# Talking-heads attention followed by a parametric-ReLU feed-forward: half of each step's feed-forward share placed ahead of the score products, four rounded-half tiles for seven relay tiles, the first input split spread over three steps

## Chip, cores and metric

The kernel runs on 1 core of one Trainium2 chip. The metric is the device time of one launch in microseconds (us), the median of several runs.

## What is computed

Four batches, 12 heads, 448 tokens, head size 64; then a feed-forward over 1792 tokens with 768 model and 2048 hidden features. The inputs q, k and w_pre are drawn eight times larger than the other random tensors.

```
def _attn_ref(q, k, v, w_pre, w_post):
    scale = 1.0 / np.sqrt(q.shape[-1])
    scores = scale * np.matmul(q, k.transpose(0, 1, 3, 2))
    scores = np.einsum('bhij,hg->bgij', scores, w_pre)
    scores = scores - np.max(scores, axis=-1, keepdims=True)
    attn = np.exp(scores)
    attn = attn / (np.sum(attn, axis=-1, keepdims=True) + 1e-09)
    attn = np.einsum('bhij,hg->bgij', attn, w_post)
    return np.matmul(attn, v).astype(np.float32)

def _moe_ref(x, w_in, w_out, alpha):
    h = x @ w_in
    g = np.maximum(h, 0.0) + alpha * np.minimum(h, 0.0)
    return (g @ w_out).astype(np.float32)
```

The feed-forward's x is the attention's output with heads side by side. `w_in` and `w_out` come as 64-bit floats.

## The kernel before

There are two phases: attention, and the feed-forward. Attention goes in 90 steps. Queries are cut into 32 chunks of 60 rows (30 at a batch's end); a chunk has 6 (or 3) groups of 10 rows over 12 heads, and a step treats two groups. A step `n` (`step`, line 595) issues, in this order:

- `mix(n)` (L209): the pre-softmax head mixing, 8 matmuls on TensorE from two relay tiles `sr` into a pair of PSUM banks; then the row maximum `nm` on VectorE (L211).
- `relays` (L202): SyncE copies score rows from the chunk's tile `st` into a ring of 8 relay tiles `sr`, two DMAs a group. A tile is refilled when the mix that read it has ended.
- `flush`: SyncE stores finished output rows `xe` to the scratch `x2` in DRAM (L271).
- `norm(n-1)` on VectorE (L567 to L571); every sixth step or so `pv` (L254), the product with v; `post(n-2)` (L231), the post-softmax mixing, 56 matmuls, copied by ScalarE to `at` (L237).
- `exp(n)` on ScalarE (L218).
- one or two score products `qk` (L186) of a chunk some steps ahead, copied by ScalarE to `st` (L190), and the loads of q and k on ScalarE's queue.
- `moe_work`: a share of the feed-forward, in two halves, with `converts` behind each.

The share is set by `PACE`: 2000 modelled ns a step while the first batch's feed-forward runs, 5400 after it. `moe(t)` is a generator; each `next` issues 3 matmuls of the first layer (L409) or 12 of the second (L443) and returns a cost from 207 ns a matmul. The feed-forward of the first batch begins at step 29. What is left of it when the steps end runs alone.

The weights are float64 and are rounded to float32 on the chip in 64 units of 128x384 (`convert`, `round_f64`, lines 51 to 68), each in five instructions' worth of `next`: exponent mask on VectorE (L61); clamp and scale of the exponent on GpSimd (L62, L63) and mantissa mask on VectorE (L65); and three more on VectorE (L66 to L68). The result lies in a tile `ct`, of which there are 3, and GpSimd stores it to the scratch `wsc` (L297). That store is issued when the unit two later does its clamp, and behind the clamp:

```
            for j, op in enumerate(round_f64(nc, raw, e, t)):
                op()
                if j == 1 and shut:
                    shut.pop(0)()
                if j == 4:
                    shut.append(close)
                yield
```

A unit's tile is first written at L65, so VectorE stops there until the store of the unit three earlier has landed. The feed-forward loads `wr` back from `wsc` (L339); ScalarE rounds it (L352) and GpSimd subtracts (L353), which gives the two parts `ws` of a weight. `load_w` runs conversions ahead of their turn when its weight is not stored yet.

The feed-forward's input is read back from `x2` in six pieces `xr` of 128x448 (two buffers, SyncE, L459), each split by two VectorE instructions into `xs` (L472, L473). For the first batch all six are split at the end of step 27.

PSUM is four pairs of banks; a group takes the pair that was freed longest ago. Every engine works its own list in order, and SyncE's and ScalarE's DMA issues stand in those lists too.

Of the kernel before, what the change touches and what calls it, by code (L numbers as in the profile page):

```python
# [10 lines left out]
I32 = mybir.dt.int32  # L11
# [17 lines left out]
NCC = DM // 128  # L29
# [2 lines left out]
NS = 4  # L32
NJ = S // 64
SR0 = 4
RA = 4
QA = 3
NSR = 2 * RA
WARM = 12
LAG = 2
TB = [(b * S, S) for b in range(B)]  # L40
# [2 lines left out]
AW = 2 * CW  # L43
FG = 2
NG2 = NFC // FG
PACE = (2000.0, 5400.0, 5400.0)
CU = DM // 2
CONV_LEAD, CONV_T0 = 4, 4


def round_f64(nc, raw, e, t):

    w = raw.bitcast(I32).rearrange("p (n t) -> p n t", t=2)
    lo, hi = w[:, :, 0], w[:, :, 1]
    tf = t.bitcast(F32)
    v, g = nc.vector, nc.gpsimd

    yield lambda: v.tensor_scalar(out=e, in0=hi, scalar1=0x7FF00000, scalar2=None, op0=ALU.bitwise_and)  # L61
    g_clamp = lambda: g.tensor_scalar(out=e, in0=e, scalar1=float(1150 << 20), scalar2=float(916 << 20), op0=ALU.min, op1=ALU.max)  # L62
    g_scale = lambda: g.tensor_scalar(out=e, in0=e, scalar1=float(-(916 << 20)), scalar2=8.0, op0=ALU.add, op1=ALU.mult)  # L63
    yield lambda: (g_clamp(), g_scale(),
                   v.tensor_scalar(out=t, in0=hi, scalar1=0xFFFFF, scalar2=0x100000, op0=ALU.bitwise_and, op1=ALU.bitwise_or))  # L65
    yield lambda: v.scalar_tensor_tensor(out=tf, in0=lo.bitcast(U32), scalar=2.0 ** -32, in1=t, op0=ALU.mult, op1=ALU.add)  # L66
    yield lambda: v.scalar_tensor_tensor(out=e, in0=hi, scalar=-0x80000000, in1=e, op0=ALU.bitwise_and, op1=ALU.bitwise_or)
    yield lambda: v.tensor_tensor(tf, tf, e.bitcast(F32), ALU.mult)  # L68
# [3 lines left out]
def talking_heads_prelu(ctx: ExitStack, tc: tile.TileContext, q, k, v, w_pre, w_post, mask, w_in, w_out, alpha, out):  # L72
# [141 lines left out]
    def exp(n):  # L214
        e_t[n] = ep.tile([128, 2, S], F32, tag="e", name=f"e{n}")
        se_t[n] = sm.tile([128, 2], F32, tag="se", name=f"se{n}")
        for u in range(2):
            nc.scalar.activation(out=e_t[n][:, u], in_=m_t[n][:, u, :S], func=AF.Exp, bias=nm_t[n][:, u:u + 1], scale=1.0,  # L218
                                 accum_out=se_t[n][:, u:u + 1])
        free(m_t.pop(n))  # L220
# [59 lines left out]
    def convert():  # L280
        todo = [(f, x, c) for f in range(NFC) for x in range(2) for c in range(0, DM, CU)]
        raw_c, shut = {}, []

        def fetch_c(i):
            if i < len(todo):
                f, x, c = todo[i]
                raw_c[i] = cvp.tile([128, CU], I64, tag="cr", bufs=4, name=f"cr{f}_{x}_{c}")
                nc.gpsimd.dma_start(out=raw_c[i], in_=(w_in, w_out)[x][f, :, c:c + CU])

        def unit(i):  # L290
            f, x, c = todo[i]
            raw = raw_c.pop(i)
            e = cvp.tile([128, CU], I32, tag="ce", name=f"ce{f}_{x}_{c}")
            t = cvp.tile([128, CU], I32, tag="ct", bufs=3, name=f"ct{f}_{x}_{c}")
            def close():
                stored.add((f, x, c))
                nc.gpsimd.dma_start(out=wsc[f, :, x * DM + c:x * DM + c + CU], in_=t.bitcast(F32))  # L297
                fetch_c(i + 4)

            for j, op in enumerate(round_f64(nc, raw, e, t)):  # L300
                op()
                if j == 1 and shut:
                    shut.pop(0)()
                if j == 4:
                    shut.append(close)
                yield

        for i in range(2):
            fetch_c(i)
        yield  # L310
        n = len(todo)
        seq = []
        for i in range(n + 1):
            seq += [(i, 0), (i, 1), (i, 2)] if i < n else []
            seq += [(i - 1, 3), (i - 1, 4)] if i else []
        units = {}
        for i, j in seq:
            if j == 0:
                units[i] = unit(i)
            next(units[i], None)  # L320
            if i < 2 and j == 1:
                fetch_c(i + 2)
            yield
        for f in shut:
            f()


    wr_t, wi_t, wo_t, g_t, xs_t, xr_t = {}, {}, {}, {}, {}, {}
# [133 lines left out]
    def split_x(t):  # L462
        a, N = TB[t]
        while step_now[0] < ready[t] + 1:
            yield
        for c in range(2):
            if (t, c) not in xr_t:
                load_x(t, c)
        xs = xs_t[t] = xsp.tile([128, 2, NCC, N], F32R, tag="xs", name=f"xs{t}")
        for c in range(NCC):  # L470
            xr = xr_t.pop((t, c))
            nc.vector.tensor_copy(xs[:, 0, c, :], xr[:, :N])  # L472
            nc.vector.tensor_tensor(xs[:, 1, c, :], xr[:, :N], xs[:, 0, c, :], ALU.subtract)  # L473
            if c + 2 < NCC:
                load_x(t, c + 2)
            yield
# [20 lines left out]
    with tc.manual_schedule():  # L497
# [45 lines left out]
        def relays(upto, dmas):  # L543
            nonlocal relayed
            while relayed < min(upto, NG) and (groups[relayed][0], NP // 2 - 1) in done_qk:
                relay(relayed, dmas)
                relayed += 1

        relays(4, (nc.sync, nc.scalar))
        relays(2 * RA, (nc.sync,))  # L550
        next(conv)
        conv_done, conv_steps = 0, NFC * 2 * 5 * (DM // CU) + 1
        tasks = [None] * len(TB)
# [3 lines left out]
        def converts(n):  # L557
            nonlocal conv_done
            for _ in range(n):
                if conv_done < conv_steps:  # L560
                    next(conv, None)
                    conv_done += 1
# [12 lines left out]
        def moe_work(n, amount):  # L575
            nonlocal cur, budget
            budget += amount
            while budget > 0 and cur < len(TB):
                if tasks[cur] is None:
                    if n <= ready[cur] + 2:  # L580
                        budget = 0.0
                        return
                    for _ in (nxt_x[cur] if cur in nxt_x else split_x(cur)):
                        pass
                    if cur == 1:
                        converts(conv_steps)
                        cvs.close()
                        wops.append(ctx.enter_context(tc.tile_pool(name="wop2", bufs=2, reuse_waits="tile")))
                    tasks[cur] = moe(cur)
                try:  # L590
                    budget -= next(tasks[cur])
                except StopIteration:
                    cur += 1

        def step(n):
            step_now[0] = n
            due = pv_at.get(n)
            lead = n <= ready[0] + 2
            pace = 0.0 if lead else PACE[min(cur, 2)]
            if live(n):  # L600
                mix(n)
            if n >= 0:
                relays(2 * (n + RA + 1), (nc.sync,))
            flush()
            if live(n - 1):
                norm(n - 1)
            if due is not None:
                b = pvs[due][0]
                for hx in range(2):
                    pv(due, hx)  # L610
                    if due + 1 < len(pvs) and pvs[due + 1][0] != b:
                        load_v(b + 1, hx)
            if live(n - LAG):
                post(n - LAG)
            if live(n):
                exp(n)
            for ci, p in qk_at.get(n, []):
                b = chunks[ci][0]
                qk(ci, p)
                if ci + 1 < NC and chunks[ci + 1][0] != b:  # L620
                    load_k(b + 1, p)
                if p == 2 and ci + 3 < NC:
                    load_q(ci + 3)
            if n in (-1, 0):
                load_q(n + 3)
            if n in (2, 3):
                load_v(0, n - 2)
            if lead:
                converts(CONV_LEAD)
            else:  # L630
                moe_work(n, pace * 0.5)
                converts(CONV_T0 // 2 + n % 2)
                moe_work(n, pace * 0.5)
                converts(CONV_T0 - CONV_T0 // 2)
            for t in range(len(TB)):
                if n == ready[t] and t == 0:
                    load_x(t, 0)
                    load_x(t, 1)
                if n == ready[t] + 1 and t == 0:
                    for _ in split_x(0):  # L640
                        pass
                    nxt_x[0] = iter(())
            if n == ready[0] - 5:
                ahead(1)
                for u in range(2):
                    load_w(u, 1)
            if n == ready[0] - 2:
                for u in range(2):
                    split_w(u, 0)
                ahead(2)  # L650
# [43 lines left out]
```

## Time and profile before

| what | us |
|---|---|
| runs | 987.4 median of 3, 985.16 to 995.29 |
| profiled execution, its time | 984.49 |
| its span, first to last instruction | 982.7 |
| TensorE matmul busy | 856.1 (87%) |
| VectorE busy | 611.3 (62%) |
| GpSimd busy | 460.2 (47%) |
| ScalarE busy | 428.8 (44%) |

PE is TensorE, PEld its weight loads, DVE VectorE, ACT ScalarE, POOL GpSimd, SP SyncE; a q behind a name is its queue of DMA issues. A row of the timeline has start, length, engine, line, operation, tiles, count, and in brackets the idle time before it and what ended that. L12 is line 12 of the kernel. The attention steps reach from 22 to 634 us, and the feed-forward is mixed into them from 204 us on; from 634 us it runs alone.

### The profile page before, as it was taken

How to read it: one execution, taken by the hardware profiler on the slowest of the kernel's cores; microseconds unless marked ns; L12 is line 12 of the kernel's file. 1: busy time of each engine (PE TensorE's matmuls, PEld its weight loads, DVE VectorE, ACT ScalarE, POOL GpSimd, SP SyncE). 2: the span in 40 equal slices, each digit the busy share in tenths (PEclk: the TensorE clock that was granted, in tenths of full speed). 3: DMA queues.
4: the chain of work that ended last, by engine and by line, in shares of the span. 5: the costliest groups of instructions: out<-in, count | busy, mean ns of one | idle time of the engine just before them, and what ended most of it. 6: DMA issues, size and time to landing. Idle time of an engine off the chain costs nothing.

```text
span 982.7 us, 27239 instructions
## 1 busy us (share of the span) xinstructions
PE 856.1 (87%) x11532; PEld 670.0 (68%) x11532; DVE 611.3 (62%) x1079; ACT 428.8 (44%) x780; POOL 460.2 (47%) x532
## 2 busy tenths in 40 slices
PE   5688595488896889787989979999999999999997
PEld 2465364266574566555657758899988999889997
DVE  4468674488947686864846556546466465765464
ACT  2367483365564456453556645423323223133231
POOL 5224243137444455536330310666555766567661
PEclk8779897889999989899889989999999999999999
DMA  6677957767865865685574542443345443454322
GB/s 183 174 223 231 244 160 249 240 174 218 227 186 172 245 208 169 204 241 173 176 195 124 156 145 101 120 125 113 97 132 166 125 115 106 126 161 116 110 81 73
DMA packets 84234, 161.71 MB, mean 165 GB/s; under 512 B 27300, under 2 KB 68720, under 8 KB 84112
## 3 DMA queue, kind: packets, MB, share of 16 engines
q0 software_dynamic: 19968, 88.36, 31.9%
q1 hardware_dynamic: 48216, 55.59, 17.8%
q10 hardware_dynamic: 15928, 16.01, 6.4%
q8 instruction: 91, 1.49, 0.7%
q14 instruction: 31, 0.25, 0.1%
HBM read 97.62 MB, written 23.59 MB: 123 GB/s over the span
## 4 chain that ended last, share of the span: by engine, by line
PE 52%; DMA 16%; DVE 14%; issue 6%; POOL 6%; ACT 4%; ACTq 1%; SPq 1%; POOLq 0%; DVEq 0%
PE p L409 19%; PE p L443 17%; DMA sr<-st 7%; PE p L254 5%; PE p L231 5%; PE p L186 4%; POOL ws L353 4%; PE p L209 3%; DMA x<-xe 3%; DMA wsc<-ct 3%; DVE nm L211 2%; ACT e L218 2%; DVE acc L375 2%; DMA xr<-x 1%; DMA k<-in_k_dram 1%
## 5 line engine op out<-in xcount | busy, mean ns | idle before, releaser
L353 POOL TENSOR_TENSOR ws<-wr,ws 128x768 fp32r<-128x768 f32 x128 | 236.6, 1849 | 274.3 <-ACT ws L352 273.4
L443 PE MATMUL p<-g,ws 128*128 128x448 f32 x1152 | 250.2, 372 | 15.4 <-DVE t L361 6.9
L409 PE MATMUL p<-xs,ws 128*128 128x448 f32 x1152 | 250.8, 371 | 1.8 <-POOL ws L353 0.8
L443 PEld LDWEIGHTS p<-g,ws 128*128 128x128 f32 x1152 | 217.1, 190 | 47.1 <-DVE t L361 8.6
L409 PEld LDWEIGHTS p<-xs,ws 128*128 128x128 f32 x1152 | 214.0, 189 | 43.7 <-issue 18.5
L352 ACT CAST ws<-wr 128x768 fp32r<-128x768 f32 x128 | 104.1, 837 | 207.2 <-issue 117.0
L231 PEld LDWEIGHTS p<-r,e 64*64 64x64 f32 x5040 | 112.4, 148 | 79.4 <-ACT at L237 29.1
L231 PE MATMUL p<-r,e 64*64 64x60 f32 x5040 | 116.9, 236 | 36.3 <-ACT at L237 20.4
L218 ACT ACTIVATE e<-p,nm 128x448 f32<-128x448 f32 x180 | 112.9, 636 | 72.7 <-DVE nm L211 64.2
L237 ACT COPY at<-p 128x960 f32<-128x960 f32 x88 | 86.8, 986 | 118.9 <-PE p L231 67.7
L209 PE MATMUL p<-sr,wk 64*64 64x448 f32 (+1 forms) x720 | 103.6, 609 | 35.6 <-DMA sr<-st 11.0
L360 DVE TENSOR_SCALAR t<-p,alpha_sb 128x448 f32<-128x448 f32 x64 | 43.5, 679 | 143.2 <-PE p L409 143.2
L211 DVE TENSOR_REDUCE nm<-p 128x2 f32<-128x896 f32 x90 | 97.7, 1085 | 47.9 <-PE p L209 47.5
L186 PE MATMUL p<-k,q 64*64 64x448 f32 x768 | 110.3, 618 | 14.6 <-ACT at L237 6.1
L62 POOL TENSOR_SCALAR ce<-ce 128x384 int32<-128x384 int32 x64 | 34.8, 543 | 180.4 <-DVE ce L61 178.8
L375 DVE TENSOR_TENSOR acc<-p,acc 128x896 f32<-128x896 f32 x84 | 90.6, 1085 | 36.6 <-PE p L443 33.5
L254 PEld LDWEIGHTS p<-at,v 64*64 64x64 f32 x2688 | 79.2, 138 | 26.8 <-ACT e L218 20.1
L254 PE MATMUL p<-at,v 64*64 64x120 f32 (+1 forms) x2688 | 82.3, 269 | 16.3 <-ACT e L218 15.8
L339 POOL DMA_DIRECT2D wr<-wsc x128 | 71.9, 562 | 43.0 <-POOL ws L353 30.3
L190 ACT COPY st<-p 128x896 f32<-128x896 f32 x95 | 84.8, 915 | 13.0 <-PE p L186 6.9
L209 PEld LDWEIGHTS p<-sr,wk 64*64 64x64 f32 (+1 forms) x720 | 26.2, 142 | 74.8 <-ACT e L218 15.4
L367 DVE TENSOR_TENSOR g<-t,g 128x448 fp32r<-128x448 f32 x64 | 73.0, 1181 | 0.9 <-ACT g L366 0.9
(45 smaller groups left out, 591.4 us busy)
## 6 DMA issues: line engine op xcount, KB each, us to landing
wr<-wsc POOLq DMA_DIRECT2D x128, 384.0 KB, 3.4
sr<-st SPq DMA_DIRECT2D x356, 105.0 KB
cr<-in_w_in_dram POOLq DMA_DIRECT2D x32, 384.0 KB, 5.3
cr<-in_w_out_dram POOLq DMA_DIRECT2D x32, 384.0 KB, 5.1
wsc<-ct POOLq DMA_DIRECT2D x64, 192.0 KB, 3.9
xr<-x SPq DMA_DIRECT2D x24, 224.0 KB
out_dram<-acc SPq DMA_DIRECT2D x12, 448.0 KB
q<-in_q_dram ACTq DMA_DIRECT2D x53, 90.0 KB
```

The costliest lines, as they stand in the source:

```text
L186: nc.tensor.matmul(pt[64 * cc:64 * cc + 64, r, :S], q_t[ci][h, (3 * cc + p) * cn + (64 - cn) * cc:(3 * cc + p) * cn + (64 - cn) * cc + 64] ...
L209: nc.tensor.matmul(to[hf:hf + 64, u, :S], wk[r, :], g[r, :], start=True, stop=True)
L211: nc.vector.tensor_reduce(out=nm, in_=to[:, :, :S], axis=AX.X, op=ALU.max, negate=True)
L218: nc.scalar.activation(out=e_t[n][:, u], in_=m_t[n][:, u, :S], func=AF.Exp, bias=nm_t[n][:, u:u + 1], scale=1.0, accum_out=se_t[n][:, u:u ...
L231: nc.tensor.matmul(dst[:, :, HI * u:HI * u + HI], e[h, u, 64 * jb:64 * jb + 64], r[h, u].rearrange("p (h i) -> p h i", h=H), start=True, s ...
L237: nc.scalar.copy(at[:, :, col:col + 2 * GI].rearrange("p q (g i) -> p g q i", g=2), pt[:, :, :NS * GP].rearrange("p g (q i) -> p g q i", i ...
L254: nc.tensor.matmul(to[64 * t:64 * t + 64, r, cl * cn:(cl + 1) * cn], v_t[b, hx][pr, s, (2 * cl + t) * D:(2 * cl + t + 1) * D], a_t[pr, s, ...
L352: nc.scalar.copy(t[:, 0], w)
L353: nc.gpsimd.tensor_tensor(t[:, 1], w, t[:, 0], ALU.subtract)
L375: nc.vector.tensor_tensor(dst, pt[:, :, :N], dst, ALU.add)
L409: nc.tensor.matmul(pt[:, f % 2, :S], w[:, tw, c * 128:(c + 1) * 128], xs[:, tx, c, :], start=(j == 0), stop=(j == 3 * NCC - 1))
L443: nc.tensor.matmul(pt[:, d, :S], w[:, tw, (c + d) * 128:(c + d + 1) * 128], g[:, tg], start=(j == 0), stop=(j == 3 * FG - 1))
```

## The change

The relay ring has 7 tiles instead of 8, and step n asks for groups up to 2n+8 instead of 2n+9; `ct` has 4 tiles instead of 3; the store of a rounded unit stands ahead of the later unit's clamp, its next fetch behind it; PACE is 2100 for the first batch; the first feed-forward starts at step 30; half of a step's share stands between `post`/`exp` and `qk`, the other half behind `qk`; two of the conversions stand ahead of `qk`; the six pieces of the first input are split two each in steps 27, 28 and 29.

```diff
-RA = 4
-NSR = 2 * RA
+NSR = 7
-PACE = (2000.0, 5400.0, 5400.0)
+PACE = (2100.0, 5400.0, 5400.0)
...
-            t = cvp.tile([128, CU], I32, tag="ct", bufs=3, name=f"ct{f}_{x}_{c}")
+            t = cvp.tile([128, CU], I32, tag="ct", bufs=4, name=f"ct{f}_{x}_{c}")
             def close():
                 stored.add((f, x, c))
                 nc.gpsimd.dma_start(out=wsc[f, :, x * DM + c:x * DM + c + CU], in_=t.bitcast(F32))
+                yield
                 fetch_c(i + 4)
+                yield
 
             for j, op in enumerate(round_f64(nc, raw, e, t)):
+                if j == 1 and shut:
+                    next(shut[0])
                 op()
                 if j == 1 and shut:
-                    shut.pop(0)()
+                    next(shut.pop(0))
                 if j == 4:
-                    shut.append(close)
+                    shut.append(close())
...
-        relays(2 * RA, (nc.sync,))
+        relays(NSR, (nc.sync,))
...
-                    if n <= ready[cur] + 2:
+                    if n <= ready[cur] + 3:
...
-            lead = n <= ready[0] + 2
+            lead = n <= ready[0] + 3
...
-                relays(2 * (n + RA + 1), (nc.sync,))
+                relays(2 * (n + 1) + NSR, (nc.sync,))
...
             if live(n):
                 exp(n)
+            if not lead:
+                moe_work(n, pace * 0.5)
+            converts(CONV_LEAD // 2)
             for ci, p in qk_at.get(n, []):
...
-            if lead:
-                converts(CONV_LEAD)
-            else:
+            if not lead:
                 moe_work(n, pace * 0.5)
-                converts(CONV_T0 // 2 + n % 2)
-                moe_work(n, pace * 0.5)
-                converts(CONV_T0 - CONV_T0 // 2)
+            converts(CONV_LEAD // 2 + (0 if lead else n % 2))
...
-                if n == ready[t] + 1 and t == 0:
-                    for _ in split_x(0):
-                        pass
-                    nxt_x[0] = iter(())
+                if ready[t] < n <= ready[t] + 3 and t == 0:
+                    split0 = nxt_x.setdefault(0, split_x(0))
+                    for _ in range(NCC // 3):
+                        next(split0)
```

`ready[0]` is 26. Line numbers of the changed kernel differ by a few; in the pieces of its order below L208 is the mix, L230 post, L185 the score product, L412 the first layer, L210 the row maximum, L475 and L476 the split, L296 the store of a rounded unit, L61 and L62 its clamp and scale, and L287 the fetch.

On TensorE in step 31, before:

```order
L209 MATMUL p_130<-sr_123,wk 64x448 x2
L209 MATMUL p_130<-sr_124,wk 64x448 x2
L231 MATMUL p_132<-r_2696,e_2651 64x12x5 x28
L186 MATMUL p_131<-k_1_1410,q_126 64x448 x4
L409 MATMUL p_133<-xs_2426,ws_0_2120 128x448 x9
```

and in the same step now:

```order
L208 MATMUL p_131<-sr_123,wk 64x448 x2
L208 MATMUL p_131<-sr_117,wk 64x448 x2
L230 MATMUL p_132<-r_2674,e_2643 64x12x5 x28
L412 MATMUL p_129<-xs_2422,ws_0_2113 128x448 x6
L185 MATMUL p_130<-k_1_1413,q_125 64x448 x4
L412 MATMUL p_129<-xs_2422,ws_0_2116 128x448 x3
```

Six of the nine first-layer matmuls moved ahead of the score product (sr_117 to sr_124 are the relay tiles, now to sr_123, and p_129 to p_133 are PSUM pairs).

On GpSimd in the attention phase, one unit's pass, before:

```order
L62 TENSOR_SCALAR ce_1_0_1051<-ce_1_0_1051 128x384
L63 TENSOR_SCALAR ce_1_0_1051<-ce_1_0_1051 128x384
L297 DMA wsc<-ct_0_0_868 128x384
L288 DMA cr_0_0_1058<-in_w_in_dram 128x384
L62 TENSOR_SCALAR ce_1_384_1126<-ce_1_384_1126 128x384
```

and now:

```order
L296 DMA wsc<-ct_0_0_864 128x384
L61 TENSOR_SCALAR ce_1_0_1042<-ce_1_0_1042 128x384
L62 TENSOR_SCALAR ce_1_0_1042<-ce_1_0_1042 128x384
L287 DMA cr_0_0_1049<-in_w_in_dram 128x384
L296 DMA wsc<-ct_0_384_932 128x384
```

The store of the unit two earlier moved ahead of the clamp and scale; the fetch stayed behind them.

On VectorE from the end of step 27, before:

```order
L472 CAST xs_2426<-xr_0_2348 128x448
L473 TENSOR_TENSOR xs_2426<-xr_0_2348,xs_2426 128x448
L472 CAST xs_2426<-xr_1_2350 128x448
L473 TENSOR_TENSOR xs_2426<-xr_1_2350,xs_2426 128x448
L472 CAST xs_2426<-xr_2_2429 128x448
L473 TENSOR_TENSOR xs_2426<-xr_2_2429,xs_2426 128x448
L472 CAST xs_2426<-xr_3_2433 128x448
L473 TENSOR_TENSOR xs_2426<-xr_3_2433,xs_2426 128x448
L472 CAST xs_2426<-xr_4_2437 128x448
L473 TENSOR_TENSOR xs_2426<-xr_4_2437,xs_2426 128x448
L472 CAST xs_2426<-xr_5_2441 128x448
L473 TENSOR_TENSOR xs_2426<-xr_5_2441,xs_2426 128x448
```

and now, with the next row maximum in view:

```order
L475 CAST xs_2422<-xr_0_2346 128x448
L476 TENSOR_TENSOR xs_2422<-xr_0_2346,xs_2422 128x448
L475 CAST xs_2422<-xr_1_2348 128x448
L476 TENSOR_TENSOR xs_2422<-xr_1_2348,xs_2422 128x448
L210 TENSOR_REDUCE nm_2435<-p_131 128x2
L570 TENSOR_SCALAR s_2441<-se_2397 128x2
L571 RECIPROCAL s_2441<-s_2441 128x2
L574 TENSOR_TENSOR r_2444<-wq,s_2441 128x120
```

Two pieces stand ahead of step 28's row maximum instead of six.

## Rows read from the trace of the kernel before

**Rows 1.** Stretches: length, busy PE, PEld, DVE, ACT, POOL, PEclk, DMA share, GB/s
```profile
22.00:178.00 156.00, 114.70 (x2570) 73.63 (x2567) 97.09 (x223) 88.38 (x178) 52.11 (x89) 0.83 0.75 219
178.00:204.00 26.00, 12.52 (x361) 9.28 (x353) 15.36 (x37) 8.43 (x18) 5.78 (x11) 0.79 0.60 185
204.00:634.00 430.00, 375.75 (x6847) 270.43 (x6851) 289.06 (x565) 233.21 (x448) 176.96 (x232) 0.94 0.62 181
634.00:983.00 349.00, 340.35 (x1723) 310.12 (x1714) 201.22 (x230) 94.79 (x134) 211.73 (x174) 1.00 0.41 118
```

**Rows 2.** The chain that ended last, after 634 us: start, length, what
```profile
641.51 7.44 PE p L409 x36
```

**Rows 3.** Waits of VectorE from 204 to 634 us: total, times, longest
```profile
DVE ct L65 <- DMA wsc<-ct: 40.6, 13, 8.0
```

**Rows 4.** Timeline, VectorE at the first and last of four long waits
```profile
297.06 0.36 DVE L65 TENSOR_SCALAR ct<-cr 128x384 int32<-128x384 int32 x1 [8.03 <-DMA wsc<-ct]
...
465.31 0.36 DVE L65 TENSOR_SCALAR ct<-cr 128x384 int32<-128x384 int32 x1 [6.51 <-DMA wsc<-ct]
```

**Rows 5.** Timeline, TensorE ahead of and behind these waits
```profile
290.75 0.98 PE L209 MATMUL p<-sr,wk 64*64 64x448 f32 x8
291.55 1.04 PE L231 MATMUL p<-r,e 64*64 64x60 f32 x54
...
301.50 1.77 PE L209 MATMUL p<-sr,wk 64*64 64x448 f32 x8 [4.26 <-ACT e L218]
303.05 1.91 PE L231 MATMUL p<-r,e 64*64 64x60 f32 x56
...
310.30 1.09 PE L231 MATMUL p<-r,e 64*64 64x60 f32 x54 [2.83 <-DVE r L571]
...
344.80 1.86 PE L231 MATMUL p<-r,e 64*64 64x60 f32 x54 [5.10 <-ACT e L218]
...
397.34 1.77 PE L209 MATMUL p<-sr,wk 64*64 64x448 f32 x8 [3.76 <-ACT e L218]
...
468.23 2.24 PE L443 MATMUL p<-g,ws 128*128 128x448 f32 x5 [6.91 <-DVE t L361]
```

**Rows 6.** Timeline, GpSimd ahead of the first of them
```profile
289.42 0.51 POOL L62 TENSOR_SCALAR ce<-ce 128x384 int32<-128x384 int32 x1
290.01 0.52 POOL L63 TENSOR_SCALAR ce<-ce 128x384 int32<-128x384 int32 x1
290.58 0.59 POOL L297 DMA_DIRECT2D wsc<-ct  x1
```

**Rows 7.** Timeline, the split of the first input
```profile
184.96 0.63 DVE L473 TENSOR_TENSOR xs<-xr,xs 128x448 fp32r<-128x448 f32 x1
...
188.00 5.50 SPq L459 DMA_DIRECT2D xr<-x  x4
191.13 0.40 DVE L472 CAST xs<-xr 128x448 fp32r<-128x448 f32 x1 [5.55 <-DMA xr<-x]
...
199.55 3.41 PE L254 MATMUL p<-at,v 64*64 64x90 f32 x81 [12.03 <-ACT e L218]
...
207.65 1.09 DVE L211 TENSOR_REDUCE nm<-p 128x2 f32<-128x896 f32 x1 [1.13 <-PE p L209]
```

**Rows 8.** Timeline, VectorE beside a subtraction of GpSimd
```profile
230.50 2.03 POOL L353 TENSOR_TENSOR ws<-wr,ws 128x768 fp32r<-128x768 f32 x1 [4.01 <-ACT ws L352]
230.72 2.23 DVE L67 SCALAR_TENSOR_TENSOR ce<-cr,ce 128x384 int32<-128x384 int32 x1
232.98 0.56 DVE L68 TENSOR_TENSOR ct<-ct,ce 128x384 f32<-128x384 f32 x1
```

**Rows 9.** Waits of TensorE from 204 to 634 us: total, times, longest
```profile
PE p L443 <- ACT ws L352: 3.4, 1, 3.4
...
PE p L186 <- ACT at L237: 2.5, 7, 0.5
```

**Rows 10.** Timeline, SyncE's relay issues; waits of TensorE from 22 to 178 us
```profile
61.63 17.59 SPq L202 DMA_DIRECT2D sr<-st  x20
...
PE p L209 <- DMA sr<-st: 7.0, 3, 3.5
```

More of the change, by code (lines that the diff above doesn't have):

```diff
@@ L324, in convert @@
         for f in shut:
-            f()
+            next(f)
     wr_t, wi_t, wo_t, g_t, xs_t, xr_t = {}, {}, {}, {}, {}, {}
```

## Prediction

> **What bounds the kernel now.** I read four stretches first, then the chain, then who waits, then the timeline at the longest waits. From 634 us on, TensorE is busy 340.35 of 349.00 us at a granted clock of 1.00, which is 2.4 GHz [rows 1]; 36 matmuls of the feed-forward take 7.44 us there, 0.207 each [rows 2]. So a feed-forward matmul costs the same 0.207 us wherever it is put, and the end comes earlier only if TensorE idles less, or runs at its higher clock more, before 634 us. There it is busy 114.70 of 156.00 us, 12.52 of 26.00 and 375.75 of 430.00, at granted clocks of 0.83, 0.79 and 0.94 [rows 1]: 54 us idle in the mixed stretch alone, though VectorE is busy for only 289.06 us of it and GpSimd for 176.96. No engine is full; work in lists that run in order is held up by single waits.
>
> Two waits stand out. VectorE stops at L65 for the store of an earlier rounded unit, 13 times, 40.6 us [rows 3]. Behind it in VectorE's list stand row maxima, norms and activations that TensorE needs: four such stops, the first 8.03 and the last 6.51 us long [rows 4], are followed by TensorE gaps of 4.26 and 2.83, 5.10, 3.76 and 6.91 us, 22.86 together [rows 5]. The second place is the split of the first input. All six pieces stand ahead of step 28's row maximum, the second load is issued only at 188.00, VectorE waits 5.55 us for it, and TensorE stands still for 12.03 us [rows 7].
>
> **The change part by part.** First the split. The second piece is done at 184.96 + 0.63 = 185.6 [rows 7], and step 28's row maximum can now follow there. The next loads stood behind SyncE's relays until 188.00 and landed by 191.13, 3.1 us later [rows 7]. One relayed group fewer stands ahead, two DMAs of 17.59 / 20 = 0.88 us [rows 10], so they go out near 186.2 and land near 189.3. Step 28 has about 3.7 us of VectorE work (1.09 row maximum, some 0.6 of norm, four conversions of about half a us, the 0.56 of rows 8 being one): 189.3. Two pieces at 1.03 (0.40 + 0.63) end near 191.4; step 29's 3.7, some 1.2 of output additions and two more pieces end near 198.4. There step 30's row maximum may start, which before came at 207.65 [rows 7]: 9.2 us sooner. But step 29 no longer does its 12 feed-forward matmuls, 12 x 0.207 = 2.5 us that come later. The net is 6.7; I take 7. Bounds: 0 if the loads land so late that each step waits, 12 if the whole gap of rows 7 goes.
>
> Second, the fourth `ct` tile. With three, unit i waits for the store of unit i-3, which GpSimd issues while it treats unit i-1; with four there is one unit more between. A unit is five conversion instructions at 4.5 a step, and the 61 mixed steps take 430 / 61 = 7.05 us: 1.11 steps, 7.8 us more time. Of the 13 waits only the longest, 8.0, exceeds that [rows 3], so nearly all should vanish. The store also goes ahead of clamp and scale, 0.51 + 0.52 us sooner [rows 6]. What is late next? L67 needs the same unit's clamp, which stood behind GpSimd's subtraction until 289.42 and was done with its scale at 290.53 [rows 6], while L65 got its tile only at 297.06 [rows 4]. VectorE ended its work ahead of L65 at 297.06 - 8.03 = 289.03, and L65 and L66 take about 0.9, so L67 would wait under 1 us. I leave 1.5 us in each of the first four gaps, which also pays for VectorE now running beside GpSimd. In the fifth I leave 4: `load_w` forces conversions ahead of an activation there, and the changed program's order has 14 conversion instructions between two row maxima where before has 11; their work remains though the store's wait goes. Saved: 22.86 - 4 x 1.5 - 4 = 12.9 us.
>
> Idle time also costs clock. Ahead of the first wait the mix takes 0.98 us and post 1.04; behind the gap 1.77 and 1.91 [rows 5], 0.79 + 0.87 = 1.66 more, as at the lower level of 1.2 GHz. Three gaps shrink so far that this should go (behind 4.26, 5.10 and 3.76): 5 us. The second part comes to 18 us. Bounds: 0 if another wait takes the place at once; 32 if all 22.86 us go, with 1.66 for each of five gaps and a little from the other, shorter waits.
>
> On the clash of VectorE with GpSimd the rows are plain: L67 took 2.23 us beside a subtraction of 2.03 us, and its neighbour L68, after it, 0.56 [rows 8]. In the Trainium skill, "GPSIMD Engine Reference", section "Specifications", GpSimd's SBUF interfaces are shared with VectorE, with contention for VectorE instructions in a two-port mode or with two SBUF inputs. The trace agrees: L67 has two. It speaks against the change: part of the subtractions now run while VectorE waits anyway, and would meet live work. It has its own case below.
>
> Third, half of the share ahead of the scores. Between one mix and the next the work is the same, so what hides `exp` is the same. What can gain is a score product that waits for the `at` copy: 2.5 us in 7 waits [rows 9]. What can lose is a second-layer matmul that waits for its weights, 3.4 us in one wait [rows 9], with the scores now behind it in TensorE's list. ScalarE's weight casts come ahead of the score copy, and relays behind that copy come later; but no mix in the mixed stretch is released by a relay, and half of the casts would have stood behind it in the step anyway. I take 0; bounds 3 gained, 6 lost (two such waits).
>
> Fourth, seven relay tiles. SyncE's issues bound the fast early steps: 0.88 us each, four a step, 3.5 us [rows 10]. A tile fewer matters only if SyncE comes round to it before its mix has ended. In the early stretch mixes waited 7.0 us for relays, 3 times [rows 10], for the first copies of a chunk and not for a free tile. I take 0; bounds 2 us gained, 38 lost (a rival). PACE 2100 and the start at step 30 shift matmuls of equal price: 0, cover being the full engine after 634 us; the order has 51 matmuls fewer behind the last row maximum (1671 for 1722), so 10.6 us less tail for as much more in the steps.
>
> The sum: 984.5 (profiled execution: span 982.7 and 1.8 around it) - 7 - 18 = 959.5. The median of the runs is 987.4, 2.9 above the profiled one; with it the forecast is 962.4 us.
>
> **The rivals.** *The clamp takes the store's place.* GpSimd's queue is the common cause, and L67 would wait two instructions later for the same subtraction. For it: the clamp and the store lie 1.2 us apart on GpSimd [rows 6]. Against: 6.5 us of the first wait, from 290.58 to 297.06, is the store's own flight, which L67 doesn't have. Only the split would pay: 987.4 - 7 = 980.
>
> *The clash eats the gain.* A clash cost L67 2.23 - 0.56 = 1.67 us [rows 8]. If one comes in the place of every second of the 13 waits that go, and reaches TensorE in full, 6.5 x 1.67 = 10.9 of 25 us are lost: 987.4 - 25 + 10.9 = 973. Against: only two-input steps from SBUF were long, and not every delay of VectorE reaches TensorE.
>
> *More goes than I count.* Shorter waits of rows 3 fall out too, and the clock rises over the mixed stretch: 32 + 12 - 3 (for what overlaps) = 41 off, 946.
>
> *Slower: the ring runs dry.* Place: the 28 steps ahead of the feed-forward. The second group of a step may now be asked for only three steps ahead. Three of the fastest steps are 3 x 3.5 = 10.5 us, of which SyncE's own four issues take 3.5; if a relay's flight outlasts the remaining 7 us, the mix waits in every such step. At 1.35 us in each of 28 steps the loss is 38 us: 987.4 - 25 + 38 = 1000. It decides from 1.25 us a step on (35 us: the gain of 25 and 1%). For it: the engines of DMA are at a share of 0.75 there [rows 1]. Against: half of the groups keep almost all of their lead, and slow steps give 5 to 10 us each.
>
> **How the numbers follow.** My forecast 0.56, the clamp 0.14, the clash 0.12, more 0.10, the ring 0.08. A measurement of this kernel tells about 1% from no change (977.5 to 997.3). Faster by more: 0.56 + 0.12 + 0.10 = 0.78. Within: 0.14. Slower: 0.08. The range goes from 942, a little under the case of more, to 986, above the clamp's case with 6 us for the third part's bound; outside lie the ring and the far ends.
>
> **What would show it.** Right: VectorE's wait at L64 of the changed kernel (L65 before) falls from 40.6 us to under 8; no TensorE gap over 4 us follows one; step 30's row maximum comes near 198; attention ends 24 to 28 us sooner when the moved matmuls are counted; the tail keeps 0.207 us a matmul. Wrong: a new VectorE wait for GpSimd's scale of 3 us or more; VectorE's two-input rows over 2 us more often than before; mixes before 178 us that wait for relays for over 15 us; or a tail that is no longer full.

## Result and profile after

The changed kernel takes 959.75 us, median of 4 runs (957.81 to 960.42); the kernel before takes 986.28, median of 4 (985.02 to 995.29). The ratio is 0.9711, with a 95% interval of 0.966 to 0.9762: 2.9% or 28 us faster (the two medians lie 26.5 us apart). The forecast was 962.4 in a range of 942 to 986. The profiled execution took 957.81 us with a span of 956.0.

Here are the same four stretches of the changed kernel as in [rows 1], with the same columns.

```profile
22.00:178.00 156.00, 111.99 (x2609) 70.94 (x2608) 98.37 (x229) 88.81 (x178) 54.48 (x92) 0.86 0.75 221
178.00:204.00 26.00, 17.86 (x426) 12.48 (x430) 17.83 (x41) 12.78 (x28) 6.57 (x11) 0.83 0.71 214
204.00:634.00 430.00, 396.35 (x6931) 289.43 (x6924) 298.54 (x566) 235.34 (x448) 193.14 (x242) 0.96 0.64 187
634.00:983.00 349.00, 313.23 (x1522) 284.82 (x1521) 188.44 (x216) 87.34 (x123) 194.91 (x160) 1.00 0.37 107
```

TensorE is busy for 396 instead of 376 us of the third stretch, at a granted clock of 0.96 instead of 0.94, and for 18 instead of 12.5 us of the second. The span ends at 956, so the last row covers 322 us. VectorE has done a little more in the third stretch, not less: what went is its waiting. These are its three longest waits there and one short one, which answer to [rows 3]:

```profile
DVE nm L210 <- PE p L208: 33.9, 20, 5.9
DVE acc L378 <- PE p L446: 31.1, 15, 9.9
DVE xe L267 <- ACT xe L266: 28.5, 19, 8.8
...
DVE ce L66 <- POOL ce L62: 0.4, 1, 0.4
```

No row of `ct <- DMA wsc` is left: 40.6 us in 13 waits became none. VectorE now waits for TensorE and ScalarE, which is idle time of an engine that is ahead. The last row is the one that the clamp's rival needed: 0.4 us.

The split of the first input, on VectorE, SyncE and TensorE, which answers to [rows 7]:

```profile
184.20 0.40 DVE L475 CAST xs<-xr 128x448 fp32r<-128x448 f32 x1 [5.17 <-DMA xr<-x]
...
186.14 1.08 DVE L210 TENSOR_REDUCE nm<-p 128x2 f32<-128x896 f32 x1
190.63 0.50 DVE L475 CAST xs<-xr 128x448 fp32r<-128x448 f32 x1 [1.09 <-DMA xr<-x]
...
198.53 0.39 DVE L475 CAST xs<-xr 128x448 fp32r<-128x448 f32 x1 [0.50 <-DMA xr<-x]
...
200.96 1.08 DVE L210 TENSOR_REDUCE nm<-p 128x2 f32<-128x896 f32 x1
```

```profile
186.52 2.25 SPq L462 DMA_DIRECT2D xr<-x  x2
```

```profile
181.58 1.77 PE L208 MATMUL p<-sr,wk 64*64 64x448 f32 x8 [7.06 <-ACT at L236]
195.29 0.98 PE L208 MATMUL p<-sr,wk 64*64 64x448 f32 x8 [3.01 <-DVE xe L267]
```

Step 28's row maximum follows two pieces at 186.14 (197.04 before), the second loads go out at 186.52 (188.00 before), and step 30's row maximum starts at 200.96 instead of 207.65. The gap of 12.03 us is gone; a gap of 7.06 stands ahead, and one of 3.01 behind.

To compare stretches of kernels that do different amounts of feed-forward per step I take the start of a step's row maximum and subtract 0.2066 us (7.44 / 36, [rows 2]) for every feed-forward matmul begun before it. Worked out from the profiled executions, in us:

```
step                27     30     48     64     84     89   end of span (2304 matmuls)
before           178.4  205.2  292.4  373.2  466.1  490.3   506.7
after            173.6  198.5  276.6  353.4  449.3  464.0   480.0
alone: ring      177.9  204.5  299.8  380.8  468.4  491.7   507.3
  tile + ring    177.5  209.6  296.2  377.7  459.4  483.0   497.1
  split          178.9  201.2  293.1  377.0  472.9  497.6   514.3
  halves         181.4  211.2  299.1  379.6  473.9  498.1   512.2
after, 3 tiles   178.3  199.3  286.1  374.6  471.2  485.9   499.4
after, at once, step 29
                 177.6  207.2  297.8  381.5  477.1  492.4   505.0
after, at once, step 30
                 172.5  205.3  283.9  359.1  456.2  471.0   484.8
after, two steps, step 29
                 178.0  208.4  293.1  373.6  468.3  483.6   496.0
```

The changed kernel gains 6.7 us by step 30, another 9.1 by step 48 and 4.0 by step 64; it loses 3.0 again by step 84 and gains 9.5 between steps 84 and 89, 26.3 in all at the last step. The tail behind it is the same 16 us beyond the matmuls' own time. Of the first 6.7 us, 4.8 were there at step 27, ahead of the split. In all the executions of this study the row maximum of step 27 starts somewhere between 172.5 and 181.4, also in kernels whose order is almost the same up to there. So a difference of that size in one column of this table proves little; the ratios below do the deciding.

### The profile page after: what moved, and what is told of

Same layout as the page of the kernel before. It is cut to its first block, busy times and chain, and to the rows that moved or that the text cites. A ratio compares the mean times of both kernels' runs of the same rounds, so it can differ in the third digit from the quotient of the medians.

```text
span 956.0 us, 27282 instructions
## 1 busy us (share of the span) xinstructions
PE 855.0 (89%) x11532; PEld 665.0 (70%) x11532; DVE 612.6 (64%) x1078; ACT 428.4 (45%) x780; POOL 462.7 (48%) x532
## 4 chain that ended last, share of the span: by engine, by line
PE 63%; DMA 16%; DVE 13%; ACT 3%; issue 2%; POOL 2%; ACTq 1%; SPq 1%; POOLq 0%; DVEq 0%
PE p L412 22%; PE p L446 19%; DMA sr<-st 9%; PE p L253 6%; PE p L230 6%; PE p L208 5%; PE p L185 4%; DMA xr<-x 2%; DVE nm L210 2%; DMA x<-xe 2%; DVE acc L378 2%; DVE xs L476 1%; ACT e L217 1%; DMA k<-in_k_dram 1%; POOL ws L356 1%
## 5 line engine op out<-in xcount | busy, mean ns | idle before, releaser
L412 PE MATMUL p<-xs,ws 128*128 128x448 f32 x1152 | 255.8, 372 | 1.4 <-DVE xs L475 0.6
L412 PEld LDWEIGHTS p<-xs,ws 128*128 128x128 f32 x1152 | 211.3, 188 | 39.8 <-issue 15.7
L230 PEld LDWEIGHTS p<-r,e 64*64 64x64 f32 x5040 | 106.3, 141 | 84.5 <-issue 30.5
L230 PE MATMUL p<-r,e 64*64 64x60 f32 x5040 | 112.1, 230 | 40.1 <-ACT at L236 17.6
L210 DVE TENSOR_REDUCE nm<-p 128x2 f32<-128x896 f32 x90 | 97.7, 1085 | 71.4 <-PE p L208 53.3
L208 PE MATMUL p<-sr,wk 64*64 64x448 f32 (+1 forms) x720 | 103.4, 600 | 31.6 <-ACT at L236 14.0
L185 PE MATMUL p<-k,q 64*64 64x448 f32 x768 | 106.8, 606 | 8.7 <-ACT at L236 3.7
L296 POOL DMA_DIRECT2D wsc<-ct x64 | 35.4, 553 | 135.4 <-DVE ct L67 135.3
L208 PEld LDWEIGHTS p<-sr,wk 64*64 64x64 f32 (+1 forms) x720 | 27.9, 141 | 72.3 <-issue 27.1
```

The costliest lines, as they stand in the source:

```text
L185: nc.tensor.matmul(pt[64 * cc:64 * cc + 64, r, :S], q_t[ci][h, (3 * cc + p) * cn + (64 - cn) * cc:(3 * cc + p) * cn + (64 - cn) * cc + 64] ...
L208: nc.tensor.matmul(to[hf:hf + 64, u, :S], wk[r, :], g[r, :], start=True, stop=True)
L210: nc.vector.tensor_reduce(out=nm, in_=to[:, :, :S], axis=AX.X, op=ALU.max, negate=True)
L230: nc.tensor.matmul(dst[:, :, HI * u:HI * u + HI], e[h, u, 64 * jb:64 * jb + 64], r[h, u].rearrange("p (h i) -> p h i", h=H), start=True, s ...
L412: nc.tensor.matmul(pt[:, f % 2, :S], w[:, tw, c * 128:(c + 1) * 128], xs[:, tx, c, :], start=(j == 0), stop=(j == 3 * NCC - 1))
```

## Experiments

All ratios are to the kernel before, with their 95% intervals. Four edits were put into the kernel before, alone; four were taken out of the changed kernel; four more followed.

**Seven relay tiles alone** (`a_ring7`).

```diff
-NSR = 2 * RA
+NSR = 7
-                relays(2 * (n + RA + 1), (nc.sync,))
+                relays(2 * (n + 1) + NSR, (nc.sync,))
```

> The kernel before with one edit, seven relay tiles instead of eight and relays asked for one group later. Theory (the ring is not what binds): 986 us, within 3 of before, and mixes ahead of 178 us wait for relays about 7 us as before. Rival (the ring runs dry): slower by 10 us or more, with waits of mixes for relays over 15 us.

Measured: 986.71 us, 0.9975 (0.995 to 1.0001). TensorE's wait for relays from 22 to 178 us:

```profile
PE p L208 <- DMA sr<-st: 6.0, 3, 2.2
```

6.0 us for 7.0 before [rows 10]. The ring's eighth tile was worth nothing, and the slow rival fell. Giving it up costs nothing, and makes the room for the fourth rounded-half tile.

**The fourth rounded-half tile, with the seven relay tiles that make room** (`a_ct4_ring7`).

```diff
-            t = cvp.tile([128, CU], I32, tag="ct", bufs=3, name=f"ct{f}_{x}_{c}")
+            t = cvp.tile([128, CU], I32, tag="ct", bufs=4, name=f"ct{f}_{x}_{c}")
```

> The kernel before with seven relay tiles and the fourth rounded-half tile (eight relay tiles and four of those don't fit together). Theory (the store's flight held VectorE): VectorE's wait for the store falls from 40.6 us in the mixed stretch to under 8, and the time by 18 us to about 968. Rival 1 (another wait takes the place): the wait goes, the time stays within 5 us of before. Rival 2 (the order of the halves is what pays): time within 5 us of before too, and the kernel with the halves alone is faster by 15 us or more.

Measured: 972.1 us, 0.9816 (0.9776 to 0.9856): 1.84% or 18 us (16 by the medians), the size that was forecast. VectorE's waits in the mixed stretch have no row of the store any more; the first and the fifth of their rows are

```profile
DVE nm L210 <- PE p L208: 31.6, 15, 8.3
...
DVE ce L60 <- DMA cr<-in_w_out_dram: 8.6, 4, 2.8
```

The second is new: VectorE, running further ahead, now waits at times for the raw weight to arrive, 8.6 us for 40.6.

**The split over three steps, alone** (`a_split`): the last hunk of the diff, and the two bounds raised from `+ 2` to `+ 3`.

> The kernel before with one edit, the first input's split spread over steps 27 to 29 and the feed-forward begun at step 30. Theory: TensorE's gap of 12 us at 187 us goes, 7 us off, about 979. Rival: the loads of each step only wait in other places and the later start costs as much: within 2 us of before.

Measured: 989.93 us, 0.9997 (0.9965 to 1.003), a miss. In the table 4 us are gained at step 30 and nothing is left of them at step 48. In the mixed stretch the store's wait is still there, and one gap of TensorE is longer than any in the mixed stretch of the kernel before:

```profile
DVE ct L65 <- DMA wsc<-ct: 30.1, 10, 5.4
```

```profile
PE p L443 <- DVE t L361: 10.5, 1, 10.5
```

This gap begins at 467 us, at the conversions that are forced in step 66, and is 3.6 us longer than the fifth gap of [rows 5]. But the split's gain is gone by step 48, ahead of it. So in this program the gain was lost again in the stretch where the stores hold VectorE. That the stores take it back is not shown, and `c_pair` below speaks against it: no wait for a store is left there, and the split adds nothing either.

**Half of the share and two conversions ahead of the scores, alone** (`a_half`).

```diff
+            if not lead:
+                moe_work(n, pace * 0.5)
+            converts(CONV_LEAD // 2)
             for ci, p in qk_at.get(n, []):
```

> The kernel before with one edit, half of the feed-forward share and two conversions ahead of the score products. Theory: 0, within 5 us of before (981 to 991). Rival: the waits of score products and mixes for copies by ScalarE are what the change removes, 15 us off or more.

Measured: 989.92 us, 1.0025 (0.9997 to 1.0053). Nothing, as forecast.

The four parts alone give 0.25%, 1.84% (with the ring), 0.03% and -0.25%, against 2.9% together. Without the interplay that is 1.84 + 0.03 - 0.25 = 1.62%, 16 us; some 12 us (give or take 8, by the intervals) are in how they meet, or in what was not tried alone (pace, place of the store). So parts were taken out of the changed kernel.

**Without the fourth tile** (`b_ct3`): `bufs=3` in the changed kernel.

> The changed kernel with three rounded-half tiles again. Theory (the fourth tile carries most of the gain, the rest needs it): the store's wait comes back with 30 us or more in the mixed stretch and the time rises to 980 or more. Rival (the parts add up as measured alone): about 16 us over the changed kernel, 976.

Measured: 971.59 us, 0.9809 (0.9764 to 0.9855), 1.0% over the changed kernel. The wait is back,

```profile
DVE ct L64 <- DMA wsc<-ct: 28.8, 12, 5.4
```

but it costs less than in the kernel before; neither expectation hit. In the table this kernel loses 9.5 us to the changed one by step 48, of which 4.7 were there at step 27, and 21 by step 64; its profiled execution is the slowest of its four (977.14).

**Without the split and the later start** (`b_nosplit`): the edits of `a_split` undone.

> The changed kernel with the first input split at once in step 27 and the feed-forward begun at step 29 again. Theory (the split's 7 us are kept once VectorE no longer stops for the store): 7 us slower, about 967. Rival (the split is worth nothing, as it was alone): within 2 us of the changed kernel.

Measured: 977.94 us, 0.9889 (0.9837 to 0.9942): 1.8% or 18 us slower than the changed kernel. What is worth nothing alone is the largest single part here, and more than its 7 us. The edit has two halves: where the pieces are split, and that the feed-forward begins one step later.

**Split at once in step 27, start at step 30** (`c_once_start30`).

```diff
-                if ready[t] < n <= ready[t] + 3 and t == 0:
-                    split0 = nxt_x.setdefault(0, split_x(0))
-                    for _ in range(NCC // 3):
-                        next(split0)
+                if n == ready[t] + 1 and t == 0:
+                    for _ in split_x(0):
+                        pass
+                    nxt_x[0] = iter(())
```

> The changed kernel with the first input split at once in step 27, and the feed-forward still begun at step 30. Theory (what the kernel without the split lost is mostly the early start, whose weights are wanted sooner than the conversions come): 7 us over the changed kernel, 967. Rival (the split itself is worth the 17 us): 975 or more.

Measured: 965.15 us, 0.9774 (0.972 to 0.9829): 0.6% or 6 us over the changed kernel. Its gap is the old one,

```profile
198.55 3.71 PE L253 MATMUL p<-at,v 64*64 64x90 f32 x81 [9.96 <-ACT e L217]
```

and it is 6.8 us behind at step 30, 7.0 at the last step and 4.8 at the end of the span. The ratio's interval overlaps with the changed kernel's, so the size is the traces' more than the ratio's. They bear it out: from step 27 to step 30, by the table's measure, the seven executions with the split over three steps take 21.0 to 25.8 us (23.5 in the mean), and the six with the split at once 26.6 to 32.8 (29.6). So the spread split gains some 6 us between these steps.

The kernel without the split (`b_nosplit`) and this one differ in one thing, the step at which the feed-forward begins. Their ratios are 0.9889 (0.9837 to 0.9942) for step 29 and 0.9774 (0.972 to 0.9829) for step 30, and the intervals don't meet: the later start alone is worth 1.15% or 11 us here. In the table, whose two executions lie 20 us apart at the end, 12 us come between steps 30 and 48 and 8 more by step 64.

**Split over two steps, start at step 29** (`c_two_start29`).

```diff
-                    if n <= ready[cur] + 3:
+                    if n <= ready[cur] + 2:
-            lead = n <= ready[0] + 3
+            lead = n <= ready[0] + 2
-                if ready[t] < n <= ready[t] + 3 and t == 0:
+                if ready[t] < n <= ready[t] + 2 and t == 0:
-                    for _ in range(NCC // 3):
+                    for _ in range(NCC // 2):
```

> The changed kernel with the split over two steps, three pieces each, and the feed-forward begun at step 29, so that conversions are forced in three bursts (8, 11 and 12 a step) instead of two (9 and 14). Theory (the early start costs): 8 to 12 us over the changed kernel, 968 to 972. Rival (the split itself is what counts): within 3 us of the changed kernel.

Measured: 975.66 us, 0.989 (0.9854 to 0.9926): 1.8% slower than the changed kernel, more than expected. It is no faster than the split at once with the same start (0.9889), so at this start spreading over two steps gives nothing that can be seen, and the start's 11 us are most of the loss. Two rows of its TensorE show a piece of it:

```profile
195.44 3.46 PE L253 MATMUL p<-at,v 64*64 64x90 f32 x81 [4.37 <-ACT e L217]
205.70 3.47 PE L412 MATMUL p<-xs,ws 128*128 128x448 f32 x9 [5.80 <-DVE xe L267]
```

The product with v falls in step 29 too, and the first feed-forward matmuls behind it wait 5.80 us. The loss is 9.9 us at step 30, of which 4.4 were there at step 27, and 16.5 at step 48. The conversions come in three bursts, of 8, 11 and 12 in steps 49, 57 and 64 (counted as VectorE's conversion instructions between two row maxima, of which four or five are usual), instead of two; the loss up to step 48 lies ahead of all three.

**Without the halves** (`b_nohalf`): both `moe_work` calls behind the score products again.

> The changed kernel with both halves of the feed-forward share behind the score products again. Theory (the halves are worth nothing, as alone): within 3 us of the changed kernel. Rival (they pay once the store's wait is gone, and are the 10 us that the parts alone don't explain): about 970.

Measured: 964.7 us, 0.9772 (0.9734 to 0.981): 0.6% or 6 us over the changed kernel, between the two expectations; the intervals (0.966 to 0.9762 there) overlap a little. The halves seem to pay once the rest is in place, which isn't clear of noise; alone they gave nothing.

**The store behind the clamp again** (`b_late_store`).

```diff
                 op()
                 if j == 1 and shut:
+                    next(shut[0])
                     next(shut.pop(0))
```

(and the earlier `next(shut[0])` left out.)

> The changed kernel with the store of a rounded unit behind the later unit's clamp and scale again. Theory (1 us sooner is worth nothing with four tiles): within 2 us of the changed kernel. Rival: the store feeds the weight loads too, 4 us or more slower.

Measured: 963.47 us, 0.9733 (0.9677 to 0.979): 0.2% over the changed kernel, inside both intervals. Its place can't be told from nothing.

**Split and fourth tile together** (`c_pair`): the kernel before with the edits of `a_ct4_ring7` and `a_split`.

> The kernel before with seven relay tiles, four rounded-half tiles, the split over three steps and the start at step 30; halves, pace and place of the store as before. Theory (split and fourth tile help each other: the split's gain was given back at the store's waits): 25 us off, about 963. Rival (alone they gave 18 and 0, and add up): 970 or more.

Measured: 970.59 us, 0.9833 (0.9786 to 0.988), against 0.9816 with the tile alone. The theory that these two help each other fell: the split adds nothing to the tile either. Between this kernel and the one without halves stand pace 2100 and the place of the store, and 0.6% (0.9833 and 0.9772, with intervals that overlap); the store's place was worth 0.2% by itself. Whether it is the pace or the halves that lets the split pay stays open.

**No forced conversions** (`c_conv`).

```diff
-            converts(CONV_LEAD // 2 + (0 if lead else n % 2))
+            converts(CONV_LEAD // 2 + n % 2)
```

> The changed kernel with one conversion more in every second step before the feed-forward begins, as it has after; no conversion is forced any more. Theory (the burst of 14 conversions in step 65 still holds TensorE for some 4 us, and the smaller one too): 5 us under the changed kernel, 955. Rival (VectorE's work ahead of the feed-forward is on the path there): the first 30 steps take 8 us longer and the time rises by 3 us or more.

Measured: 954.53 us, 0.9686 (0.9617 to 0.9756). The changed kernel's gap at its first burst,

```profile
383.48 6.74 PE L253 MATMUL p<-at,v 64*64 64x120 f32 x142 [4.13 <-DVE t L364]
```

has no row of its kind here: from 374 to 392 us TensorE waits for nothing. By the table's measure, worked out in the same way, this kernel goes from 314.7 at step 56 to 374.1 at step 68, 59.4 us, and the changed kernel from 307.9 to 380.3, 72.4 us. So 13 us come back where the bursts were, and 6.8 are lost ahead of step 56 (3.0 of them by step 27), by the higher rate of conversions there or by the spread of single executions. The ratio is the lowest of the study, 0.25% under the changed kernel's, but the intervals overlap widely: that it is faster isn't shown.

## Why the prediction was right

The time was 959.75 for 962.4, and the gain 28 us for 25. The main cause, the store's wait, was right; the rest of the sum came out right in part by luck. Point by point:

**The store's wait.** Right in mechanism and size: forecast 18 us, 18 measured with the ring alone, and the 40.6 us fell to nothing, not to the 8 allowed. The 7.8 us more that a fourth tile gives did cover all 13 waits. Inside the changed kernel the tile is worth 10 us, 8 less than alone. Without it 28.8 us of waits come back there and not 40.6; that the other edits had eased the same stretch is likely, but not shown.

**The split.** The local working came near: step 30's row maximum was put near 198 and came at 200.96, 6.7 us sooner than before, with the 12 matmuls done ahead of it that I had moved behind it. But 4.8 of the 6.7 were there at step 27, so it is luck that this pair shows the net that I forecast; the thirteen executions counted under `c_once_start30` give 6 for 7. As a term of the sum the split was mis-sized in kind: nothing alone (0.9997) and nothing beside the tile (0.9833 for 0.9816), and some 6 us in the changed kernel, by ratios whose intervals overlap.

**The start and the pace.** The step that failed is "PACE 2100 and the start at step 30 shift matmuls of equal price: 0". The price of a matmul is the same in either place, but one that runs where TensorE would idle takes no time from the rest. The start in step 30 is worth 11 us in the changed kernel, as `b_nosplit` and `c_once_start30` show. Where the early start loses them is known in part: in `c_two_start29` the first feed-forward matmuls wait 5.80 us, and at pace 2100 the conversions are forced in three bursts for two. But in the table 12 of the 20 us are lost ahead of the first burst, and the order of `a_split`, with a single burst (10, in step 66), is no faster than the kernel before.

The pace was never run alone, but the traces show where it acts. These are the stretches from step 84's row maximum to step 89's in four kernels, with the columns of [rows 1]: before and `c_pair`, with pace 2000, then the changed kernel and `b_nohalf`, with 2100.

```profile
577.71:610.56 32.85, 26.67 (x498) 20.38 (x500) 15.01 (x33) 13.42 (x28) 4.74 (x4) 0.84 0.40 132
562.47:597.20 34.73, 28.77 (x537) 22.35 (x537) 16.94 (x36) 13.66 (x30) 4.75 (x4) 0.85 0.37 119
563.31:594.82 31.51, 31.51 (x579) 26.26 (x571) 17.60 (x35) 16.91 (x34) 6.01 (x6) 1.00 0.40 132
572.05:603.77 31.72, 31.72 (x584) 26.48 (x579) 17.53 (x36) 16.89 (x34) 6.10 (x6) 1.00 0.39 132
```

With 2000 TensorE idles for 6 us here and runs at a granted clock of 0.84 and 0.85; with 2100 it is never idle, at a clock of 1.00. There the first batch's 576 matmuls are all begun by step 86, in the kernel before by step 88 and in `c_pair` by step 89, and the larger share of 5400 follows. By the table's measure these five steps take 23.2 to 24.8 us in all six executions with 2000, and 14.6 to 15.3 in all eight with 2100: some 9 us that the sum had at nothing. Every other edit is present in one of the six or missing from one of the eight, so this is the pace's. From step 64 to step 84 the kernels with 2100 take longer (95.5 for 90.1 us in the mean, of values that overlap), so how much of the 9 us stays in the time is open.

**The halves.** Forecast 0 with bounds 3 and 6. Alone 0.25% slower, inside an interval that reaches to nothing; in the changed kernel some 6 us gained, twice the bound, by ratios whose intervals overlap a little. Once VectorE isn't late, the place of TensorE's matmuls may decide more; that reading was not tried further.

**The relay tiles.** Right: 0.9975 alone, 6.0 us of waits for 7.0.

**The bursts.** I left 4 us in the gap that a burst of conversions causes. The changed kernel has gaps of 4.13 us at the first burst and, around the second, these two:

```profile
438.89 0.34 PE L230 MATMUL p<-r,e 64*64 64x60 f32 x8 [2.42 <-issue]
...
453.55 1.86 PE L230 MATMUL p<-r,e 64*64 64x60 f32 x54 [2.64 <-ACT e L217]
```

Without bursts the first of the three is gone, and 13 us of the stretch with it, of which the ratio keeps too little to tell from nothing.

**The rivals.** The clamp: its wait is 0.4 us, so it fell. The clash: VectorE's means with two inputs from SBUF in the mixed stretch to 500 us are

```profile
L67 DVE TENSOR_TENSOR ct<-ct,ce 128x384 f32<-128x384 f32 x40 | 26.4, 661 | 1.1
L66 DVE SCALAR_TENSOR_TENSOR ce<-cr,ce 128x384 int32<-128x384 int32 x39 | 25.2, 647 | 0.4 <-POOL ce L62 0.4
L65 DVE SCALAR_TENSOR_TENSOR ct<-cr,ct 128x384 f32<-128x384 uint32 x38 | 24.0, 632 | 1.0
```

in the changed kernel, and in the kernel before, where they are L68, L67 and L66,

```profile
L67 DVE SCALAR_TENSOR_TENSOR ce<-cr,ce 128x384 int32<-128x384 int32 x41 | 26.4, 643 | 0.0
L66 DVE SCALAR_TENSOR_TENSOR ct<-cr,ct 128x384 f32<-128x384 uint32 x40 | 26.0, 649 | 1.0
L68 DVE TENSOR_TENSOR ct<-ct,ce 128x384 f32<-128x384 f32 x40 | 22.4, 560 | 1.0
```

Only one of the three got clearly longer, 0.10 us each for 40 instructions, 4 us of VectorE in all. One sign of being wrong did come: up to 500 us, VectorE's instructions with two inputs from SBUF took over 2 us five times, for three before. So the clash is there and grew a little, but it took nothing like 10.9 us. The reading that only two-input steps were long doesn't hold either. In the kernel before, L65, which has one input and takes 0.36 us in [rows 4], took 1.63 beside a subtraction of GpSimd that ran from 346.36 to 348.18:

```profile
346.76 1.63 DVE L65 TENSOR_SCALAR ct<-cr 128x384 int32<-128x384 int32 x1 [0.62 <-DMA wsc<-ct]
```

"More goes" and "the ring runs dry" did not come.

**The sum.** That 25 came so near 28 is luck in part. The terms were 18 for the tile, 7 for the split and 0 for the rest. In the changed kernel the tile is worth about 10, the split 6, the start 11 and the halves 6: a term too high and two terms put at nothing offset each other, and these parts don't add up to 28 either.

## What to carry to other kernels

A tile that is stored by DMA is a wait in the list of the engine that fills it: count the instructions between its store and its next use against the store's flight, and find the memory where a ring is deeper than anything uses. Parts of a schedule change don't add: try each alone and each taken out, since here one edit was worth 0 alone and 18 us in company. Work that is moved at an equal price can still pay or cost: ask which idle time it leaves and which it fills. Work that a consumer can force ahead of its turn arrives as a burst: look for the bursts in the order of the program when a consumer is started earlier, though here the gain of removing them was not shown.

## What the runs showed of the hardware

The feed-forward's matmuls that run alone after attention are not quite of one price, and the price changes from one batch to another. In the kernel before, 36 of them take 7.44 us in the first batch that runs there (from 641 us, [rows 2]) and 7.30 in the two behind it. In the changed kernel they take 7.30 in the first two and 7.44 in the last. From the chains, first of the kernel before, then of the changed kernel:

```profile
777.74 7.30 PE p L409 x36
```

```profile
650.59 7.30 PE p L446 x36
869.09 7.44 PE p L412 x36
```

The granted clock is 1.00 in both tails. No run here tells why.
